# A conformer block on one core: another order of all steps, weight pieces that lie in one stretch, and 16 instead of 89 products of the unit matrix

## The chip, the core and the metric

The kernel runs on one core of one Trainium2 chip. The metric is device time in microseconds, as the median of several executions. The core has a matrix engine (TensorE, PE in the profile; its weight loads are PEld), a vector engine (VectorE, DVE), a scalar engine (ScalarE, ACT), GpSimd (POOL) and SyncE (SP), which issues all DMA transfers here. Each engine works through its own queue in order and waits for the others by semaphores.

## The reference

There are two parts. The first is attention in chunks of 32 positions, with 16 positions of left and 8 of right context and 8 memory keys for each head; the second is a gated feed-forward layer that mixes along the sequence.

```python
# attention: B, H, S, D = 4, 8, 768, 64
for c in range(24):                       # chunks of 32
    k_full = concat(mem_k, k[:, :, 32*c - 16 : 32*c + 40])    # cut at the ends
    v_full = concat(mem_v, v[:, :, 32*c - 16 : 32*c + 40])
    a = softmax(q_c @ k_full.T / 8)
    out[:, :, 32*c : 32*c + 32] = a @ v_full
x = out as (B, S, 512)
# feed-forward
h = gelu(x @ w_in)                        # 512 -> 1024, tanh form
u, v = h[..., :512], h[..., 512:]
v_n = (v - mean(v)) / sqrt(var(v) + 1e-6) * g_ln
v_s = einsum('ts,bsd->btd', w_sg, v_n) + b_sg      # along the sequence
return x + (u * v_s) @ w_out
```

The weights `w_in` and `w_out` reach the kernel as float64, w_sg as float32.

## The kernel before

**Tiles.** The 4 x 768 positions are cut into 24 tiles of 128 positions (four chunks), counted by `u` = 6 b + tt. One attention tile handles all eight heads. Three tiles make a half of a batch entry (384 positions). Products of the second part run in a split form: each operand is a pair of a rounded high part and the rest, and each product adds lo x hi, hi x lo and hi x hi (`product`), so three matmuls for each 128 x 128 block.

**Steps.** The code first defines all work as named steps in a table, each with its engine, or with two engines of which a star behind the name chooses the second. It then issues them in the order that the text `ORDER` gives. Each engine's queue, SP's included, holds its steps in just this order. A second text thus moves everything at once. The steps are:

- `q`, `k`, `v` + u: loads of a tile's queries, keys and values (SP). There are two buffers of q and of k, and three of v; a load waits until the last reader of its buffer is done.
- `S`: 64 matmul records that make the scores. `mx`, `sb`, `ex`, `sm`, `sa`, `sr`, `nm`: the softmax: maximum, subtraction (VectorE), exponential (ScalarE), sum, a small addition, reciprocal (VectorE), scaling (VectorE or GpSimd). `z` sets to zero the keys that lie outside (GpSimd).
- For the first ten tiles `T` (four transpositions on TensorE with the unit matrix) and `p` (the copy to `pt`) turn the weights around; for the others `yt` does so in blocks on VectorE, and the exchanges `Ea` to `Ed`, four transfers of 32 KB each within the chip's memory, move the blocks for two tiles at a time.
- `A`: 64 matmul records that weigh the values. `xc`, `xh`, `xl`: the copy to float32 (ScalarE), the high part (ScalarE), the rest (GpSimd or VectorE).
- `V`: the product with the second half of `w_in` for a tile (12 matmuls of 512 columns); `v1` to `v9` with `vx`, `vy`: gelu, statistics, normalisation (`v7`), the pair `vh` (`v8` on ScalarE, `v9` on GpSimd or VectorE).
- `U` + b, half, j: the product with a fourth of the first half of `w_in` (12 matmuls of 384 columns); `u1` to `u4`: its gelu.
- `W`: the product along the sequence (18 matmuls of 384 columns); it needs all six `vh` of the batch entry. `w1` to `w4`: shift, gate, the pair.
- `O`: the product with `w_out` (12 matmuls); `o1` adds x; `out` stores 192 KB.

**Weights.** A piece of `w_in` is 128 rows of 512 float64. `ri10` to `ri13` load those of the half that V needs, `ri00` to `ri03` those that U needs, `ro0` to `ro3` those of `w_out`. The steps `d1` to `d9` turn a piece into a pair of float32: `d1`, `d2` take the bits of the mantissa and the exponent apart (VectorE), `d3`, `d4` convert them (ScalarE), `d5`, `d6` add the low word and the sign (VectorE), `d7` multiplies (GpSimd or VectorE), `d8` rounds to the high part (ScalarE), `d9` subtracts it (GpSimd or VectorE). Six raw buffers serve the eight pieces of `w_in`. A V needs the pairs of all four `i1` pieces, a U those of all four `i0` pieces. `g` + st, half loads a piece of the transposed w_sg into one of seven buffers (`us`), which the U's use later; `ga` and `gb` make its pair. `cb` loads g_ln and b_sg, `cbh` halves them.

**Banks.** Four banks of PSUM (`mms`) serve T, V, U, W, O in turn; a step takes the one that has been free the longest. A V or a U holds its bank until its last gelu step. The scores and the weighted values have two banks each of their own.

**The unit matrix.** A step `zz7` issues `warm(7)`: seven products of the unit matrix with itself, into the bank that is next to be taken. Nothing reads what they write. A product of float32 is two matmul records in the profile.

**Line numbers.** All steps go through one helper, so nearly all instructions in the profile have the line L110. They are told apart by their tiles: `rawa` to `rawf`, `ma`.., `exa`.. belong to the pieces, `ea`, `eb`, `mx`, `rd` to the softmax, `paira`, `pairb` to x or to the gated product of the first and the second half, `ga`, `gb` to V, `ua` to `ug` to U and to pieces of w_sg, `vha` to `vhf` to the six vh.

Of the kernel before, what the change touches and what calls it, by code (L numbers as in the profile page):

```python
# [36 lines left out]
d2i10 g50 d5i01 d4i10 g40 sm0 S1 d6i10 g51 sa0 zz12 d7i01* g41 sr0 mx1 d8i01 d1i10 sb1 d3i10 k3 nm0 ex1
d5i10 T0 sm1 S2 p0 d9i01* A0 sa1 k4 mx2 q3 d2i12 ri11 sb2 zz12 d4i12 q4 d1i12 ex2 sr1 d6i12 d3i12 nm1* sm2
xh0 xc0 sa2 xl0 T1 d5i12 zz3 sr2 d7i10* p1 S3 nm2 d8i10 d7i12* A1 q5 d9i10* d8i12 ri13 T2 d1i11 xc1 k5 d2i11
zz9 d3i11 d9i12 mx3 xh1 p2* d4i11 sb3 xl1 S4 ex3 d5i11 zz22 d2i13 d1i13 d4i13 d6i11 d3i13 d6i13 ri03 ri00  # L40
d5i13 v2 d7i11* v4 d7i13 mx4 d8i11 sm3 sb4 d9i11 d8i13 sa3 S5 ex4 sr3 d9i13* zz2 k7 d1i03 V01 q7 mx5 nm3*
d3i03 k6 sm4 ri02 d2i00 v3 sa4 d2i03 d4i00 sr4 d5i03 d4i03 d6i00 T3 v101 A2 d6i03 p3 nm4* v201 V00 sb5 v5
xh2 q6 v301 xl2 d7i03 ex5 v401 xc2 d1i00 z5 d8i03 d1i02 d3i00 d2i02 T4 d9i03* v100 V02 sm5 d3i02 p4 v200
d4i02 d5i02 v300 sa5 d6i02 v400 A3 d7i02 sr5 v501 S6 v500 xc3 d8i02 nm5 A4 xh3 d9i02* T5 mx6 xl3 xc4 zz4 xh4
vx01 vx00 sb6 p5 V03 vy00 xl4 ex6 v600 vy01 d5i00 z6 v601 sm6 d7i00 sa6 sr6 A5 v701 d8i00 nm6 v801 V04 v700
xc5 v901* xh5 d9i00 v102 xl5 v800 v202 ga50 v900* v302 U001 gb50* v104 v402 g21 ga31 v204 ga40 gb31 ga41
v502 U003 v304 gb40* g01 ga51 gb41 v404 k8 u1001 v6 ga11 vx02 u2001 ga21 gb51 ro0 vy02 v504 T6 u3001 q8
u1003 S7 cb u4001 v602 ga20 vx04 gb21 u2003 p6 U000 vy04 mx7 ga01 v604 u3003 sb7 gb20 u4003 ex7 V05 v704
u1000 sm7 v804 gb11* v904* sa7 v702 v103 sr7 S8 u2000 v802 nm7* v203 u3000 U011 u4000 k10 v303 v902 mx8 k9
q9 v403 g00 cbh sb8 v105 g10 T7 u1011 v503 q10 U010 ex8 v205 p7 vx03 sm8 v305 vy03 u2011 U002 v405 u3011  # L50
v603 sa8 u4011 ga00 v505 ga10 gb00 sr8 vx05 S9 vy05 v605 v703 g30 A6 mx9 gb10 v7 v803 k11 U012 sb9 xc6 q11
nm8* u1010 ex9 u2010 v903* u3010 T8 ga30 v705 S10 d1o0 v805 gb30* d3o0 A7 u4010 v905 u1012 sm9 U013 u2012
xc7 sa9 p8* u3012 u4012 d2o0 d5o0 d4o0 W001 mx10 d6o0 sb10 d7o0 ro1 sr9 ex10 gb01* d8o0 W003 nm9* w1001
u1013 sm10 u2013 d9o0 w2001 u3013 sa10 w3001 u4013 sr10 w4001* W010 w1003 u1002 d1o1 u2002 d3o1 w2003 u3002
d5o1 w3003 d2o1 u4002 w4003 T9 d4o1 w1010 W002 d6o1 w2010 d7o1 ro2 p9* v8 w3010 nm10 d8o1 w4010 W012 w1002
w2002 d9o1 w3002 d2o2 d1o2 d4o2 w4002 W011 d3o2 w1012 d6o2 d5o2 w2012 ro3 d7o2* w3012 w4012 d8o2 A8 w1011
w2011 S11 xc8 d9o2* W000 w3011 mx11 q13 v9 w4011* d1o3 d2o3 d3o3 sb11 d4o3 d5o3 ex11 W013 d6o3 z11 w1000
d7o3* w2000 d8o3 yt10 w3000 d9o3* A9 w4000* w1013 O000 sm11 w2013 sa11 w3013 sr11 nm11* O002 o1000 w4013*
yt11 Eb5 O011 o1002 O012 o1011 Ec5 O001 o1012 v10 O010 o1001 out001 Ea5 O003 o1010 k13 O013 q12 o1003 xh7
xh6 out003 xl7* xh8 v11 xl6 out000 V11 v12 o1013 k12 xl8* out002 Ed5 V12 v111 v211 out011 v311 v411 U101  # L60
v511 v112 vx11 v212 xc9 vy11 v312 v611 V10 xh9 v412 u1101 v711 u2101 v811 v512 u3101 v911 u4101 vx12 S12
vy12 xl9* v612 v110 A10 v712 k14 v210 q14 v812 V13 mx12 xc10 v310 v912* xh10 v410 xl10* sb12 V14 v113 v510
ex12 v213 z12 vx10 v313 sm12 v413 A11 sa12 vy10 v513 v610 sr12 vx13 v710 S13 xc11 vy13 nm12 v613 U100 v810
mx13 xh11 v910* sb13 xl11 v114 yt12 U103 ex13 v214 u1100 v713 v314 sm13 v813 U113 v414 u1103 v913 sa13 u2100
sr13 u2103 u3100 nm13* v514 u3103 V15 u1113 u4100 u4103 u2113 yt13 u3113 vx14 u4113 Ed6 vy14 U111 v614 v115
v714 v215 v814 v315 v914 U110 u1111 v415 u2111 v515 u3111 U112 u4111 u1110 vx15 vy15 u2110 v615 u3110 v715
u4110 S14 v815 u1112 v915* U102 q16 mx14 q15 u2112 Ea6 sb14 u3112 u4112 W113 ex14 sm14 sa14 out012 sr14 nm14
Eb6 W103 w1113 w2113 out013 w3113 v13 w4113 out010 k15 u1102 W110 v14 w1103 Ec6 u2102 w2103 u3102 w3103
u4102 w4103 k16 W101 w1110 w2110 w3110 w4110 yt14 S15 w1101 A12 w2101 q17 mx15 w3101 k17 W112 w4101* xc12
sb15 ex15 sm15 sa15 sr15 W100 nm15* w1112 w2112 yt15 w3112 w4112* W111 w1100 w2100 w3100 w4100* S16 w1111  # L70
A13 w2111 mx16 w3111 W102 w4111 Ec7 xc13 sb16 ex16 sm16 sa16 sr16 k18 nm16* v16 S17 w1102 Eb7 O110 w2102
mx17 w3102 w4102* sb17 Ea7 O103 ex17 o1110 z17 sm17 sa17 sr17 O111 o1103 nm17* q19 k19 out103 v15 O113 q18
o1111 out111 Ed7 O101 o1113 O102 o1101 yt16 S18 o1102 A14 yt17 mx18 O100 xc14 sb18 ex18 z18 A15 sm18 xh12
o1100 xh14 S19 sa18 xl12* xh13 Ec8 sr18 xl14 O112 mx19 sb19 xl13 ex19 out110 V22 o1112 nm18* out102 sm19 v17
Ea8 sa19 sr19 nm19 U202 v122 v222 out101 Ed8 v322 U200 v422 u1202 u2202 v522 u3202 q20 u4202 V21 Eb8 u1200
vx22 vy22 v622 u2200 v722 u3200 u4200 v822 v922 v18 U201 v121 out100 q21 v221 v321 U203 v421 u1201 yt18 v521
u2201 V20 xc15 yt19 u1203 vx21 xh15 vy21 u2203 v621 u3201 xl15* u3203 u4201 A16 u4203 v120 v721 v220 v821
V23 v19 xc16 v921* k21 v320 k20 xh16 v420 out112 xl16 v520 A17 vx20 v123 vy20 v620 v223 V24 Ec9 xc17 v720
v323 xh17 v423 v820 xl17 v523 v20 vx23 S20 vy23 v920 Ed9 U210 mx20 v623 v124 sb20 v224 ex20 Ea9 S21 v723
v324 sm20 v823 V25 v424 u1210 v923 sa20 u2210 sr20 v524 u3210 out113 nm20* q22 u4210 k23 vx24 mx21 k22 U212  # L80
v125 vy24 sb21 Eb9 v624 v225 ex21 v724 v325 sm21 U213 v824 v425 u1212 v924 sa21 u2212 v525 u3212 U211 sr21
u1213 u4212 nm21* vx25 u2213 vy25 yt20 u3213 v625 u4213 A18 v725 yt21 v825 S22 v21 xc18 v925 A19 mx22 sb22
W211 Ec10 xc19 ex22 sm22 sa22 sr22 nm22 Ed10 W202 w1211 Ea10 W203 w1202 w2202 w3202 q23 Eb10 w4202* u1211
u2211 W210 w1203 u3211 w2203 v22 u4211 w3203 w2211 w4203 w3211 W213 w4211* w1210 yt22 w2210 w3210 w4210*
W201 w1213 w2213 w3213 w4213* W212 w1201 w2201 w3201 w4201* W200 w1212 w2212 w3212 w4212* O213 w1200 w2200
w3200 w4200 O212 o1213 O201 o1212 out212 O203 o1201 O211 o1203 S23 o1211 A20 mx23 O200 sb23 xc20 ex23 z23
sm23 O202 o1200 sa23 out200 sr23 nm23 out211 yt23 A21 xh20 o1202 xh18 xl20 out202 O210 xh19 xl19* xl18 V32
o1210 out210 out203 Ec11 U301 v132 v232 v23 v332 out201 V30 v432 u1301 Ed11 u2301 v532 u3301 u4301 vx32 vy32
v632 Ea11 U300 v130 v732 xc21 v230 v832 v330 v932 U303 u1300 v430 Eb11 xh21 u2300 xl21 v530 u3300 V31 u4300
u1303 vx30 vy30 u2303 v630 u3303 v730 u4303 v830 v930* V33 v131 v231 v331 v431 A22 v531 v133 vx31 v233 U302  # L90
xc22 vy31 v631 v333 xh22 v731 v433 v831 xl22 A23 u1302 v533 u2302 v931 V34 vx33 xc23 vy33 u3302 v633 xh23
u4302 v733 xl23* v833 v933 V35 v134 v234 v334 v434 U310 v534 v135 vx34 v235 vy34 v335 v634 U312 v435 u1310
v734 v535 v834 u2310 v934 U313 vx35 u1312 vy35 u3310 u2312 v635 u4310 u3312 v735 U311 u4312 u1313 v835 u2313
v935* u3313 u4313 W310 W312 w1310 w2310 w3310 w4310 u1311 W302 w1312 u2311 w2312 u3311 w3312 u4311 w4312*
W301 w1302 w2302 w3302 w4302 W311 w1301 w2301 w3301 w4301* W300 w1311 w2311 w3311 w4311 W303 w1300 w2300
# [536 lines left out]
```

## Time and profile before

| what | value |
|---|---|
| median of 3 runs | 406.43 us (404.9 to 407.65) |
| the profiled execution's own time | 406.15 us |
| its span, first to last instruction | 404.4 us |
| mean granted TensorE clock in it | 0.987 |
| busy: PE, DVE, ACT, POOL | 95%, 70%, 39%, 26% of the span |
| read and written | 36.96 MB, 6.29 MB |

The profile is of one execution. Busy time of PE is from modelled ends of pipelined matmuls, and the unit matrix counts in it. A row of the timeline gives start and duration in microseconds, engine, line, operation, tiles and shapes; a wait in square brackets is the idle time of that engine before the instruction and what ended it. A row of the chain of waits gives start, duration and what was on the chain. A row of the waits gives who waited for whom, the total, the number of times and the longest. A row of DMA issues gives the number of transfers, the size of one and the median time from issue to landing.

### The profile page before, as it was taken

Reading aid. Unit: us, or ns where it says so; the run is one execution under the profiler, and the core shown is the slowest. Engines: PE = TensorE matmul, PEld = TensorE weight load, DVE = VectorE, ACT = ScalarE, POOL = GpSimd, SP = SyncE. Lnnn points to the kernel's source line nnn. Section 1 sums busy time; section 2 is a strip of 40 time slices with the busy share of each in tenths; the row PEclk is TensorE's granted clock in tenths of the full one; section 3 lists DMA queues with packets and bytes.
Section 4 is the critical chain, followed back from the end, with each engine's and each line's share of the span. In section 5 each row is a group of like instructions: output and inputs, shape, how many; then the busy total and the mean of one; then the engine's idle time right before and its main releaser. Section 6 shows DMA issues by size and latency. Waiting matters only on the chain.

```text
span 404.4 us, 11378 instructions
## 1 busy us (share of the span) xinstructions
PE 384.9 (95%) x4922; PEld 358.3 (89%) x4922; DVE 283.5 (70%) x557; ACT 159.4 (39%) x296; POOL 106.0 (26%) x114
## 2 busy tenths in 40 slices
...
PEclk9699999999999999999999999998999999999999
...
GB/s 250 369 210 202 347 4 109 202 235 60 105 134 20 192 197 65 2 75 227 109 98 200 42 171 161 177 141 86 99 0 21 62 146 18 2 1 0 2 5 172
DMA packets 24530, 47.67 MB, mean 118 GB/s; under 512 B 4384, under 2 KB 13600, under 8 KB 24480
## 3 DMA queue, kind: packets, MB, share of 16 engines
...
q8 instruction: 39, 0.64, 0.6%
q14 instruction: 11, 0.09, 0.1%
HBM read 36.96 MB, written 6.29 MB: 107 GB/s over the span
## 4 chain that ended last, share of the span: by engine, by line
PE 64%; DVE 13%; DMA 10%; SPq 4%; ACT 3%; POOL 3%; issue 2%; DVEq 0%; ACTq 0%; POOLq 0%
PE mmb L110 16%; PE mmd L110 15%; PE mma L110 13%; PE mmc L110 13%; SPq L110 4%; PE av L110 4%; PE s L110 3%; DMA rawa<-in_w_in 2%; DMA pt<-y 2%; DVE ga L110 2%; DVE gb L110 2%; DMA rawf<-in_w_in 2%; DMA out<-xa 2%; DMA vb<-in_vs 1%; DVE rda L110 1%
## 5 line engine op out<-in xcount | busy, mean ns | idle before, releaser
L110 PEld LDWEIGHTS av<-pt,vb 64*64 64x64 f32 x512 | 8.7, 135 | 7.3 <-issue 3.4
L110 PE MATMUL av<-pt,vb 64*64 64x32 f32 x512 | 9.8, 221 | 5.6 <-issue 2.6
L110 PE MATMUL s<-kb,qb 64*32 64x64 f32 x768 | 10.6, 231 | 3.6 <-DVE rda L110 3.6
L110 PE MATMUL mma<-ident 128*128 128x128 f32 x74 | 12.7, 348 | 1.4 <-POOL mhalf L110 1.4
L110 DVE SCALAR_TENSOR_TENSOR gb<-gb,mmb 128x512 f32<-128x512 f32 x14 | 9.6, 683 | 6.1 <-ACT gb L110 6.1
L110 PEld LDWEIGHTS s<-kb,qb 64*32 64x32 f32 x768 | 8.6, 109 | 5.7 <-DVE rda L110 3.8
L110 PEld LDWEIGHTS mma<-ident 128*128 128x128 f32 x74 | 12.0, 257 | 1.6 <-POOL mhalf L110 1.4
L110 PEld LDWEIGHTS s<-ka,qa 64*32 64x32 f32 x768 | 8.7, 109 | 4.5 <-DVE gb L110 1.6
L110 PE MATMUL s<-ka,qa 64*32 64x64 f32 x768 | 10.5, 230 | 1.9 <-DVE gb L110 1.2
L110 ACT COPY xa<-av 128x512 f32<-128x512 f32 x9 | 5.3, 585 | 15.7 <-PE av L110 14.5
L110 ACT ACTIVATE ga<-ga 128x512 f32<-128x512 f32 (+1 forms) x14 | 8.9, 634 | 6.4 <-DVE ga L110 6.4
L110 ACT COPY xb<-av 128x512 f32<-128x512 f32 x9 | 5.3, 585 | 14.8 <-PE av L110 13.3
L110 DVE SCALAR_TENSOR_TENSOR mmd<-mmd,g_half,b_half 128x384 f32<-128x384 f32 x8 | 5.0, 624 | 8.4 <-PE mmd L110 8.4
L110 PE MATMUL mmb<-pairb,w_out_hi 128*128 128x384 f32 x56 | 10.9, 336 | 0.0
L110 ACT ACTIVATE gb<-gb 128x512 f32<-128x512 f32 (+1 forms) x14 | 8.8, 631 | 4.9 <-DVE gb L110 4.9
L110 POOL TENSOR_TENSOR rsb<-rsb,mhalf 128x1 f32<-128x1 f32 x8 | 4.6, 578 | 23.1 <-DVE rsb L110 23.1
L110 DVE SCALAR_TENSOR_TENSOR mmc<-mmc,g_half,b_half 128x384 f32<-128x384 f32 x9 | 5.6, 619 | 6.8 <-PE mmc L110 6.8
L110 PEld LDWEIGHTS av<-pt,vc 64*64 64x64 f32 x512 | 8.3, 134 | 2.3 <-issue 0.7
L110 PE MATMUL mmb<-w_in_hi,pairb 128*128 128x512 f32 x32 | 9.1, 404 | 1.4 <-POOL pairb L110 1.4
L110 ACT ACTIVATE eb<-eb 128x512 f32<-128x512 f32 x12 | 7.6, 630 | 6.3 <-DVE eb L110 6.3
L110 DVE TENSOR_REDUCE mxa<-s 128x8 f32<-128x512 f32 x8 | 5.4, 678 | 6.4 <-PE s L110 6.4
L110 PEld LDWEIGHTS av<-pt,va 64*64 64x64 f32 x512 | 8.4, 134 | 1.6 <-issue 1.0
(557 smaller groups left out, 1287.3 us busy)
## 6 DMA issues: line engine op xcount, KB each, us to landing
...
vb<-in_vs SPq DMA_DIRECT2D x8, 512.0 KB, 4.3
va<-in_vs SPq DMA_DIRECT2D x8, 512.0 KB, 5.5
vc<-in_vs SPq DMA_DIRECT2D x8, 512.0 KB, 4.7
pt<-y SPq DMA_DIRECT2D x112, 32.0 KB, 2.3
...
```

The costliest lines, as they stand in the source:

```text
L110: return self.tc.keep_in_program_order(getattr(self.engine, name)(*args, **kw))
```

## The change

There are four edits.

1. The host lays out `w_in` as (2, 4, 128, 512) words of 64 bits and w_sg transposed as (2, 6, 128, 384), so that each piece that one transfer loads lies in one stretch of memory. Before, a piece was a window of a wider matrix: rows of 4 KB at a distance of 8 KB for `w_in`, rows of 1.5 KB at a distance of 3 KB for w_sg. Sizes and the places in the core's memory stay the same. `w_out` stays as it was; its pieces already lay in one stretch.
2. `ORDER` holds the same 1292 steps in another order. The choice of engine changes for 38 steps that get a star and 26 that lose theirs; VectorE then has 569 in place of 557 instructions.
3. The steps `zz` are five with 16 products in all, in place of nine with 89.
4. `warm` issues nothing where no bank is free at that place of the order.

The start of the two orders, in the queues of the engines that the prediction speaks of:

```text
SP before:  k0 q0 g20 ri01 g11 ri10 q1 k1 k2 v1 v0 q2 g31 ri12 g50 g40 g51 g41 k3 k4 q3 ri11 q4 q5 ri13 k5 ri03 ri00
SP after:   ri11 ri01 q0 ri13 g50 q1 g11 ri12 k0 k1 v1 g20 k2 ri10 g31 g41 v2 q2 v0 ri00 q3 k3 k4 ri02 k5 q4 ri03 v4 cb
  later:    v3 q5 g30 k6 q6 v6 v7 k8 v5 q8 q7 g10 g51 k7 g01 q9 q10 k10 g40 g21 v8 k9 g00 ro0
DVE before: mx0 d2i01 sb0 d1i01 d6i01 d2i10 d5i01 sm0 d6i10 sa0 d7i01 sr0 mx1 d1i10 sb1 nm0 d5i10 sm1 d9i01 sa1 mx2
DVE after:  d1i11 d2i11 d5i11 d2i01 d6i11 d1i01 d7i11 d6i01 d5i01 d9i11 d1i13 d2i13 d1i12 d5i13 d2i12 d6i13 d5i12 d6i12
            mx0 sb0 d9i13 mx1 sm0 sb1 d2i10 sa0 sr0 sm1 sa1 sr1 d6i10 d1i10 mx2 sb2 d5i10 d1i00 sm2 sa2 sr2 d2i00 nm2
            xl0 mx3 p2 sb3 d2i02 d9i10
PE before:  zz7 S0 zz18 S1 zz12 T0 S2 A0 zz12 T1 zz3 S3 A1 T2 zz9 S4 zz22 S5 zz2 V01 T3 A2 V00 T4 V02 A3 S6 A4 T5 zz4
            V03 A5 V04 U001 U003 T6 S7 U000 V05 S8 U011 T7 U010 U002 S9 A6 U012 T8 S10 A7 U013 W001
PE after:   S0 S1 zz7 S2 T0 zz2 T1 A0 zz2 S3 T2 A1 zz2 A2 V00 S4 V02 V01 T3 S5 A3 S6 T4 zz3 A4 V03 V04 T5 T6 A5
            U001 U003 A6 S7 U012 V05 U000 S8 U011 U002 U010 T7 U013 A7 S9 T8 W011
later PE before: V20 A16 V23 A17 V24 ... U211 A18 S22 A19 W211
later PE after:  S19 A16 U200 A17 V24 V23 ... U201 W203 A18 W200 A19 S20 W213
```

The diff, with the two texts cut:

```diff
 ORDER = """
-k0 q0 g20 zz7 ri01 g11 ri10 q1 k1 S0 zz18 k2 mx0 v1 d2i01 v0 sb0 d4i01 q2 d1i01 ex0 g31 d6i01 ri12 d3i01 z0
...
+ri11 ri01 q0 ri13 g50 q1 g11 ri12 k0 d1i11 d2i11 k1 d3i11 d4i11 d5i11 d2i01 v1 d6i11 d4i01 g20 d1i01 d7i11*
...
-            f"i{half}{kt}", w_in[kt * P:(kt + 1) * P, 1024 * half:1024 * half + 1024],
+            f"i{half}{kt}", w_in[half, kt],
...
-            eng.dma_start(us.take(key), w_sgT[st * P:(st + 1) * P, ts_])
+            eng.dma_start(us.take(key), w_sgT[th, st])
...
     def warm(n):
-        for _ in range(n):
+        for _ in range(n if mms.free else 0):
             tensor.matmul(mms.free[0][:, 0:P], ident, ident, start=True, stop=True)
...
+    w_in = np.ascontiguousarray(moe_w_in).view(np.int64).reshape(4, P, 2, 512).transpose(2, 0, 1, 3)
+    w_sgT = np.asarray(moe_w_sg).T.reshape(6, P, 2, HALF).transpose(2, 0, 1, 3)
     arrays = {
-        "qs": qs, "ks": ks, "vs": vs, "w_in": np.ascontiguousarray(moe_w_in).view(np.int64), "g_ln": moe_g_ln,
-        "w_sgT": np.asarray(moe_w_sg).T, "b_sg": moe_b_sg, "w_out": np.ascontiguousarray(moe_w_out).view(np.int64),
+        "qs": qs, "ks": ks, "vs": vs, "w_in": w_in, "g_ln": moe_g_ln,
+        "w_sgT": w_sgT, "b_sg": moe_b_sg, "w_out": np.ascontiguousarray(moe_w_out).view(np.int64),
     }
```

More of the change, by code (lines that the diff above doesn't have):

```diff
@@ L35 @@
 ORDER = """
-k0 q0 g20 zz7 ri01 g11 ri10 q1 k1 S0 zz18 k2 mx0 v1 d2i01 v0 sb0 d4i01 q2 d1i01 ex0 g31 d6i01 ri12 d3i01 z0
[L37 to L95, printed above, removed]
@@ L96 @@
-w3300 w4300* W313 w1303 w2303 w3303 w4303* O300 w1313 w2313 w3313 w4313 O303 o1300 O313 o1303 O312 o1313
-O310 o1312 out312 out213 O302 o1310 O311 o1302 out302 out303 out313 O301 o1311 out311 out310 out300 o1301
-out301
+ri11 ri01 q0 ri13 g50 q1 g11 ri12 k0 d1i11 d2i11 k1 d3i11 d4i11 d5i11 d2i01 v1 d6i11 d4i01 g20 d1i01 d7i11*
+d3i01 d6i01 d8i11 d5i01 d9i11* d1i13 d2i13 d3i13 d7i01 d4i13 d1i12 d8i01 d5i13 d3i12 d2i12 S0 d6i13 d4i12
+d5i12 k2 d6i12 ri10 g31 d7i13 mx0 g41 sb0 v2 d9i01 q2 d8i13 S1 v0 ex0 ri00 d9i13* z0 q3 zz7 k3 d7i12 mx1 sm0
@@ new lines @@
+sb1 d8i12 d2i10 ex1 d9i12 sa0 sr0 d4i10 sm1 sa1 nm0* sr1 S2 d6i10 d1i10 T0 nm1* k4 mx2 d3i10 zz2 p0 sb2
+d5i10 T1 ex2 A0 d1i00 ri02 d7i10 sm2 p1 d3i00 zz2 sa2 sr2 xh0 d2i00 S3 xc0 nm2 d8i10 xl0 T2 d4i00 k5 mx3 A1
+q4 p2* ri03 zz2 sb3 v4 xc1 d2i02 cb ex3 A2 d9i10* v3 d4i02 sm3 q5 V00 xh1 g30 d1i02 xc2 d6i00 d3i02 d6i02
+xh2 d5i02 xl1 xl2 S4 sa3 v100 sr3 d1i03 V02 d7i02 v200 k6 d3i03 q6 mx4 v300 d5i03 d8i02 nm3* sb4 v400 ex4
+V01 d9i02* v102 cbh v500 v202 vx00 sm4 v302 T3 vy00 v402 S5 sa4 v502 p3 sr4 A3 vx02 v600 mx5 nm4* vy02 sb5
@@ new lines @@
+v6 xc3 S6 ex5 d5i00 v602 xh3 T4 d2i03 z5 d7i00* zz3 d4i03 sm5 xl3 p4 mx6 d8i00 A4 sa5 v702 d9i00 sb6 V03
+v802 v7 sr5 xh4 k8 ex6 v902* v5 xc4 q8 z6 xl4 nm5* v101 q7 sm6 g10 v201 V04 sa6 d6i03 v301 sr6 v401 d7i03*
+nm6 d8i03 T5 v501 T6 d9i03* p5 p6* A5 ga50 ga30 vx01 gb50* ga20 U001 gb30* g51 ga31 gb20 vy01 k7 ga10 ga41
+g01 xc5 gb31* v601 ga11 v700 U003 xh5 v701 u1001 gb41 xl5 v801 u2001 ga51 gb11 v800 A6 u3001 v900* ga01
+u4001 v901 S7 u1003 v104 u2003 U012 xc6 mx7 q9 gb51 u3003 v204 v103 gb10 u4003 v304 v203 V05 u1012 gb01*
@@ new lines @@
+v303 v404 sb7 v504 ex7 v403 U000 vx04 u2012 v503 u3012 vy04 sm7 v604 u4012 S8 u1000 vx03 v704 U011 vy03
+u2000 v804 q10 v603 mx8 k10 u3000 v904 g40 sa7 u4000 g21 sb8 v8 U002 v105 v703 k9 u1011 sr7 v205 v803 nm7*
+u2011 v305 u3011 U010 v405 v903 ex8 u4011 v505 ga40 gb40 sm8 ga21 T7 vx05 sa8 vy05 U013 gb21* g00 v605 p7*
+ro0 u1002 sr8 u2002 v705 u3002 A7 nm8 v805 u4002 v905 S9 ga00 xc7 T8 gb00 mx9 W011 p8 sb9 u1010 d2o0 ex9
+d1o0 u2010 d4o0 sm9 d3o0 d6o0 u3010 W013 w1011 u4010 d5o0 w2011 ro1 d7o0* q11 w3011 v9 sa9 w4011 d8o0 sr9
@@ new lines @@
+W010 w1013 nm9 u1013 u2013 d9o0* u3013 u4013 d2o1 T9 w2013 d4o1 A8 d1o1 w3013 p9* d3o1 W003 d6o1 xc8 d5o1
+w1010 d7o1 ro2 w2010 w3010 w4013* d8o1 w4010 W002 w1003 d9o1* w2003 w3003 d2o2 d1o2 d4o2 w4003* W012 d3o2
+w1002 d6o2 d5o2 w2002 ro3 d7o2* k11 w3002 w4002 d8o2 S10 w1012 A9 w2012 k12 d9o2* w3012 q12 W000 mx10 w4012
+sb10 d2o3 ex10 d1o3 d4o3 sm10 d3o3 d6o3 S11 w1000 d5o3 W001 k13 w2000 mx11 w3000 d7o3* sb11 d8o3 w4000* ex11
+S12 d9o3* z11 w1001 O013 sm11 mx12 sa11 w2001 sr11 sa10 w3001 O011 nm11* sr10 o1013 nm10 w4001* O012 o1011
@@ new lines @@
+yt10 sb12 yt11 O001 ex12 o1012 Ec5 z12 sm12 sa12 sr12 O003 o1001 nm12* out013 q13 v11 O002 o1003 out003 k14
+q14 O000 o1002 S13 o1000 xh7 xh6 O010 xl7 mx13 xh8 sb13 xl8 ex13 S14 o1010 xl6* V12 out010 Ea5 sm13 mx14
+sa13 sr13 nm13 V10 Eb5 v112 v212 v312 v412 out002 U103 v512 v110 k15 q16 vx12 v210 Ed5 vy12 v310 v612 U102
+v410 u1103 u2103 v712 u3103 v10 v510 v812 q15 V11 u4103 u1102 out001 v912* out000 u2102 vx10 u3102 vy10 yt12
+v610 u4102 U101 v111 v710 sb14 v810 v211 ex14 v910* v311 U100 sm14 u1101 xc9 u2101 sa14 xh9 v411 u3101 sr14
@@ new lines @@
+A10 xl9* u1100 nm14* v511 V13 u4101 xc10 vx11 yt13 xh10 vy11 u2100 v611 u3100 xl10* u4100 A11 v711 v113 v811
+v213 V14 Ed6 xc11 v911* v313 xh11 v413 xl11* v513 Ec6 U110 v114 vx13 vy13 v613 v214 v713 v314 v813 V15 v414
+v12 u1110 v913 Ea6 v514 u2110 vx14 u3110 vy14 v614 u4110 U111 v714 v115 out012 v814 v215 out011 k16 v914
+v315 Eb6 U113 v415 u1111 u2111 v515 u3111 u4111 U112 u1113 vx15 vy15 v615 u2113 v715 u3113 u4113 v815 S15
+v915 yt14 A12 k17 mx15 W110 sb15 xc12 ex15 sm15 sa15 sr15 nm15 S16 w1110 yt15 W113 k18 mx16 v14 w2110 v13
@@ new lines @@
+sb16 w3110 w4110* ex16 u1112 sm16 W102 w1113 sa16 u2112 sr16 w2113 u3112 nm16* u4112 w3113 w4113* W112 w1102
+w2102 w3102 w4102* A13 w1112 w2112 W100 Ec7 xc13 w3112 w4112* q18 Ed7 W111 w1100 w2100 w3100 w4100* q17 v15
+W103 w1111 Eb7 w2111 w3111 w4111 Ea7 O111 w1103 w2103 w3103 w4103 O112 o1111 S17 o1112 yt16 A14 mx17 W101
+sb17 xc14 ex17 z17 sm17 sa17 sr17 nm17* S18 w1101 A15 w2101 yt17 w3101 O113 mx18 Ea8 w4101* sb18 ex18 O103
+o1113 z18 Ed8 sm18 sa18 sr18 nm18* O100 o1103 out103 O101 o1100 O102 o1101 out101 Ec8 O110 o1102 xh14 xh12
@@ new lines @@
+xl14* xh13 xl12* v17 xl13 V22 v18 o1110 v16 Eb8 U203 v122 out102 v222 k19 q19 v322 out100 V20 v422 u1203
+out110 u2203 v522 u3203 u4203 yt18 V21 vx22 v120 vy22 v622 v220 v722 v320 v822 v420 xc15 v922* S19 xh15 v520
+A16 v121 k21 xl15* vx20 U200 mx19 xc16 vy20 v221 xh16 v620 sb19 v321 xl16 ex19 v421 A17 u1200 sm19 V24 v720
+v20 xc17 v521 q20 v820 u2200 xh17 v920 vx21 sa19 u3200 vy21 sr19 u4200 nm19* V23 v124 v224 v621 xl17 yt19
+v324 Ed9 v424 v721 U210 v524 v821 vx24 v921 vy24 out111 V25 u1210 Eb9 v624 v123 u2210 v724 u3210 v223 v824
@@ new lines @@
+u4210 v323 v924* q21 U211 out112 v423 v125 Ea9 v523 v225 U212 u1211 vx23 vy23 v325 v623 u2211 v425 u3211 v19
+Ec9 v723 U202 v525 u1212 v823 u2212 vx25 v923* u3212 vy25 u4212 U213 v625 k20 u1202 u4211 out113 u2202 v725
+u3202 v825 u4202 U201 u1213 v925* u2213 u3213 W203 u4213 A18 w1203 w2203 W200 xc18 w3203 w4203* u1201 u2201
+u3201 A19 u4201 w1200 S20 w2200 xc19 W213 w3200 k22 mx20 w4200* sb20 ex20 sm20 S21 w1213 sa20 W212 w2213
+mx21 w3213 sr20 w4213* nm20 sb21 yt20 ex21 W210 w1212 sm21 w2212 sa21 w3212 sr21 nm21 w4212* W211 w1210 yt21
@@ new lines @@
+w2210 Ec10 w3210 w4210 W202 w1211 w2211 v21 Eb10 w3211 w4211 O211 w1202 Ed10 w2202 w3202 w4202* O213 o1211
+k23 Ea10 W201 o1213 q23 q22 O210 w1201 w2201 w3201 w4201 A20 o1210 S22 xc20 O200 mx22 sb22 ex22 O201 o1200
+sm22 sa22 sr22 nm22* S23 o1201 A21 out201 mx23 v22 yt22 O203 sb23 ex23 z23 O202 sm23 o1203 sa23 sr23 nm23
+O212 o1202 xh20 yt23 xh19 out202 xh18 out203 xl20* Eb11 xl19* V32 o1212 xl18 v23 out212 U302 v132 Ec11 v232
+v332 V31 v432 u1302 out213 u2302 out210 v532 u3302 out200 u4302 Ea11 vx32 vy32 v632 V30 v131 v732 v231 v832
```

9 lines of the change are left out of this document (added).

## The prediction, made before the result was known

> **What bounds the kernel now.** I read the page first, then the stretches, the chain of waits, VectorE's waits, single rows of the timeline.
>
> ```profile
> span 404.4 us, 11378 instructions
> ...
> PE 384.9 (95%) x4922; PEld 358.3 (89%) x4922; DVE 283.5 (70%) x557; ACT 159.4 (39%) x296; POOL 106.0 (26%) x114
> ...
> PEclk9699999999999999999999999998999999999999
> ```
>
> TensorE looks full, but that row counts the unit matrix and the waits inside a pipelined group. What the products need comes from pieces of the chain: in their order below a unit group, the scores S, the values A, a unit group, a transposition T, then V, U or O (12 matmuls of 384), W.
>
> ```profile
> 2.11 6.58 DMA rawf<-in_w_in
> 14.79 5.43 PE mma L110 x28
> 20.22 0.79 PE s L110 x53
> 21.01 1.06 PE av L110 x64
> 29.44 0.59 PE mmc L110 x4
> 32.83 5.11 PE mmd L110 x44
> 231.66 2.78 PE mmb L110 x12
> 359.34 3.12 PE mmd L110 x18
> 384.29 2.09 PE mmc L110 x12
> ```
>
> 24 S at 0.79, 24 A at 1.06, 10 T at 0.59, 24 V at 2.78, 64 U and O at 2.08 and 32 W at 3.12 are 350 us. The other 54 are the subject. The first V starts at 39.20 (row below), with 6 S, 2 A and 3 T done, 8.6 us: 30.6 lost. The first W starts at 93.86; the work between is 47.2 of 54.7 us: 7.5 lost. The remaining 310.5 hold 294.4 of work: 16.1 lost, 3.5 of it the last addition and store.
>
> ```profile
> 39.20 1.18 PE L110 MATMUL mmd<-w_in_hi,paira 128*128 128x512 f32 x4
> 93.86 0.33 PE L110 MATMUL mma<-w_sg_hi,vha 128*128 128x384 f32 x1
> ```
>
> So the start is what counts, and there VectorE sets the pace: it turns each float64 weight piece into two floats, beside softmax. The stretches (columns: PE, PEld, DVE, ACT, POOL busy, granted clock, DMA share, GB/s):
>
> ```profile
> 0.00:10.00 10.00, 8.60 (x114) 8.09 (x114) 1.98 (x4) 0.78 (x1) 0.77 (x8) 1.00 0.81 249
> 10.00:20.00 10.00, 6.38 (x92) 6.22 (x92) 7.74 (x17) 4.83 (x8) 0.19 (x1) 0.66 0.99 375
> 30.00:39.20 9.20, 9.19 (x196) 8.70 (x194) 9.10 (x15) 5.36 (x10) 4.98 (x5) 1.00 0.54 176
> ```
>
> VectorE is idle for 8 of the first 10 us and full from 30 on. Its waits in the first 95 us:
>
> ```profile
> DVE mxa L110 <- PE s L110: 6.4, 2, 5.9
> DVE mxc L110 <- PE s L110: 2.7, 2, 2.1
> DVE exf L110 <- DMA rawf<-in_w_in: 2.2, 1, 2.2
> DVE exf L110 <- ACT exf L110: 1.2, 1, 1.2
> DVE ua L110 <- ACT ua L110: 1.0, 1, 1.0
> ```
>
> **VectorE's queue, counted.** Starts of neighbours give the price of one when the queue is full: 0.60 for 512 columns of floats (27.99 to 28.59), 0.34 for an integer step (28.59 to 28.93), 0.11 for a small one (26.12 to 26.23), 0.47 for 384 columns (64.47 to 64.94).
>
> ```profile
> 26.12 0.20 DVE L110 RECIPROCAL rdc<-rdc 128x8 f32<-128x8 f32 x1
> 26.23 0.64 DVE L110 TENSOR_TENSOR ma<-ma,exa 128x512 f32<-128x512 f32 x1
> 27.99 0.68 DVE L110 TENSOR_TENSOR w_in_lo<-ma,w_in_hi 128x512 fp32r<-128x512 f32 x1
> 28.59 0.42 DVE L110 TENSOR_SCALAR mb<-rawb 128x512 int32<-128x512 int32 x1
> 28.93 0.42 DVE L110 TENSOR_SCALAR exb<-rawb 128x512 int32<-128x512 int32 x1
> 64.47 0.55 DVE L110 TENSOR_TENSOR w_sg_lo<-ud,w_sg_hi 128x384 fp32r<-128x384 f32 x1
> 64.94 0.68 DVE L110 SCALAR_TENSOR_TENSOR ga<-ga,mma 128x512 f32<-128x512 f32 x1
> ```
>
> Before the first V, the old order has 53 instructions on VectorE (to d9i13: 35 wide, 10 integer, 8 small), 25 us; the new one 47 (to d9i10: 28, 13, 6), 22 us. Up to v705, the last normalisation before W, the old order has 149 (85 wide, 18 of 384, 16 integer, 30 small), 68 us; the new one 148 (80, 22, 16, 30), 67 us. So the amount hardly moves; what moves is when it starts and how often it stops.
>
> ```profile
> 88.09 0.54 DVE L110 TENSOR_SCALAR ga<-ga,mvc,rsc 128x512 f32<-128x512 f32 x1
> 89.36 1.26 POOL L110 TENSOR_TENSOR vhf<-ga,vhf 128x512 fp32r<-128x512 f32 x1 [1.90 <-ACT vhf L110]
> 31.19 1.28 POOL L110 TENSOR_TENSOR paira<-xa,paira 128x512 fp32r<-128x512 f32 x1 [0.70 <-ACT paira L110]
> 31.27 1.74 DVE L110 SCALAR_TENSOR_TENSOR mb<-rawb,mb 128x512 f32<-128x512 uint32 x1
> ```
>
> The old v705 ends at 88.6, 20.7 after the bare sum. The waits above are 13.5; the other 7 are small waits and stretching beside GpSimd, as at 31.27, where a step of 0.68 took 1.74.
>
> **Part by part.** *Loads.* The first piece waited behind k0, q0 and g20, and took 6.58 us. Alone in the queue, a strided piece (rawd) and one that lies in one stretch (w_out) take:
>
> ```profile
> rawd<-in_w_in SPq DMA_DIRECT2D x1, 512.0 KB, 4.6
> y<-in_w_out SPq DMA_DIRECT2D x4, 512.0 KB, 3.3
> ```
>
> The new order issues ri11 first; at w_out's price from the first issue, about 0.7, it is there at 4.0, at rawd's at 5.3. I take 4.0, since w_out has the same rows of 4 KB and the new layout. [...] The later pieces arrive ahead of VectorE. k0 moves behind four pieces, so S0 starts near 12 instead of 4.7; its maximum has 18 instructions, 8.7 us, ahead of it on VectorE, so that is covered, though only just. w_sgT's pieces have hundreds of instructions of cover and I cost them at nothing. On SP's queue, ri10 stands behind k2, which waits for S0, and k7 behind g51, which waits for gb50. Who needs ri10 has 24 instructions ahead on VectorE (12.3 us), who needs k7 has 10 between gb50 and its own step (4.5 us): I cost both at nothing, and 2 us each if the cover is gone.
>
> *Unit matrix.* 89 products become 16. At 0.23 each (44 records in 5.11, two records a product) 73 are 17 us of TensorE, nearly all while it waited anyhow. One group was in the way: the 28 records from 14.79, at a half clock, held S2 and so the 2.1 us wait of mxc. The bounds of the removal are that gain of 2, and a loss from a colder clock (below); I take 1 us lost for the latter.
>
> *Order.* VectorE now starts at 4.0. Its waits, estimated: 1.6 for ScalarE's first answer (the table load, then d3), 2 for S1 and S2, 1.5 for the U's, as ua's row. With 7 for the rest, as GpSimd has 25 large operations there after 23, that is 16 in place of 20.7, from 11 to 21. v705 then ends at 67 + 16 = 83, and W follows when vhf is done, 2.0 later by the two rows at 88 and 89: 84.5. TensorE itself allows it: V00 at 22 + 9 = 31; of the 55 us of work that the new order has ahead of W (10 S, 8 A, 6 V, 8 U, 9 T) 4 S, 3 A and 3 T are done by then, 47 are left: 78. I take 84. Against 93.86 that is 9.9, less one S (0.79) that the new order has not done by then: **9 us**.
>
> *The later batches.* TensorE's waits after 95 us, and the W that ran cold after the idle time before it:
>
> ```profile
> PE av L110 <- ACT xa L110: 1.5, 1, 1.5
> PE mmb L110 <- POOL pairb L110: 1.4, 2, 0.8
> 275.52 4.78 PE mmd L110 x18
> ```
>
> A19 follows A18 with one S between, and waits for ScalarE to empty the bank; in the new order W200 stands between. The W behind it took 4.78 for 3.12. A V that follows its values at once waits for GpSimd; now a U or another V stands between, or VectorE does that step. Those are 4.5 us, less what new waits take: the exchanges stand between loads and stores on SP, with some 1 us of cover each at A12 and A14. I take **3 us**, from 4.5 gained to 5 lost.
>
> **Sum.** 404.4 - 9 - 3 = 392.4. The profiled execution was 406.15 for that span, 1.75 more: 394. Its 406.15 lies 0.3 under the median of 406.43, which I leave.
>
> **Rivals.** *The front gives back its gain.* The first piece comes early but VectorE loses the time again by waits for S0, k2 or GpSimd: W at 90, 3 us gained, nothing later: 403 at the most, 399 with the 3 later. For it: six edges above have under 1 us of cover. Against: a queue that starts 4.7 us earlier with the same work must lose them anew.
> *No change.* The front gains 9 and the exchanges lose it: A10, A12, A14, A16 each late by 2 us or so: 402 to 408. Against: the old order keeps S, A and E as near to each other.
> *The clock.* The row of 10 to 20 us shows it: TensorE waited 3.6 us, and the clock granted was 0.66; the 28 records cost 0.19 each there, 0.12 later. With 16 unit products left TensorE is idle up to S0. If the clock then stays at one half up to the first U, the work from V00 to there (5 V, 3 S, 4 T, 3 A, 22 us) takes 22 more, 3 of it hidden by VectorE: 413. It decides from about 16 us of work at one half. [...]
> *The change isn't what it says.* The loop makes no unit product where no bank is free, so even fewer than 16: nothing in time.
>
> **Numbers.** Forecast, 386 to 399: 0.66. Gain given back: 0.16, mostly faster still. No change: 0.10. Clock, or another loss: 0.08. The range of 386 to 403 takes in the bounds of the front (11 to 21 of lag) and the first rival. One per cent, 4 us, is about what a measurement can tell from no change: faster 0.79, same 0.12, slower 0.09.
>
> **What would show it.** VectorE's first weight step at 4 to 5 us; the first V at 29 to 33; the first W at 82 to 86; no PE wait for a value bank near the third batch's W; its clock low in one or two slices of the front and full later. I am wrong if VectorE's waits in the front add up to more than 10 us, if the first W comes after 90, or if TensorE waits for pt after 150 us.

## The result and the profile after

The changed kernel takes 394.66 us (median of 4, 393.48 to 394.84) beside 405.66 for the kernel before in the same comparison (4 runs, 404.07 to 407.65). The ratio is 0.9713, 95% interval 0.9673 to 0.9753. (A ratio, here and below, leaves out executions in a slower state, so it need not be the quotient of the medians.) The profiled execution took 393.48 us with a span of 391.7, against 406.15 and 404.4: 12.7 us less.

The page of the changed kernel, three lines:

```profile
span 391.7 us, 11059 instructions
...
PE 365.5 (93%) x4776; PEld 338.5 (86%) x4776; DVE 289.3 (74%) x569; ACT 160.5 (41%) x295; POOL 93.9 (24%) x103
...
PEclk9999999999999999999999999999999999999999
```

PE's busy time fell by 19.4 us (some 17 of them are the 73 unit products, by the prediction's price) and the span by 12.7: a busy share is no measure of what TensorE needs. The row of the clock looks perfect and isn't, as a later section shows.

The same landmarks in the timeline of the changed kernel (start, duration, instruction): VectorE's first weight step, the first V, the first W.

```profile
4.36 0.43 DVE L109 TENSOR_SCALAR mb<-rawb 128x512 int32<-128x512 int32 x1 [4.36 <-DMA rawb<-in_w_in]
```

```profile
33.49 1.19 PE L109 MATMUL mmd<-w_in_hi,paira 128*128 128x512 f32 x4
34.52 1.09 PE L109 MATMUL mmd<-w_in_lo,paira 128*128 128x512 f32 x4
```

```profile
85.40 0.42 PE L109 MATMUL mmd<-w_sg_hi,vha 128*128 128x384 f32 x1
```

The stretches of the changed kernel (PE, PEld, DVE, ACT, POOL busy, clock, DMA share, GB/s), and VectorE's longest waits in the first 95 us:

```profile
0.00:10.00 10.00, 0.00 (x0) 0.00 (x0) 5.28 (x11) 4.47 (x6) 1.44 (x9) 1.00 0.81 304
10.00:20.00 10.00, 4.05 (x136) 3.64 (x137) 8.98 (x14) 4.99 (x8) 6.44 (x6) 1.00 0.96 343
```

```profile
DVE mb L109 <- DMA rawb<-in_w_in: 4.4, 1, 4.4
DVE mxb L109 <- PE s L109: 0.7, 1, 0.7
DVE vha L109 <- ACT vha L109: 0.6, 1, 0.6
```

VectorE is busy for 5.3 of the first 10 us instead of 2.0, and TensorE does nothing at all in them. The old waits of 6.4, 2.7 and 2.2 us are gone; what is left behind the first piece is one of 0.7 and smaller ones.

TensorE's waits after 95 us were 4.8 us in five rows (1.5, 1.4, 0.9, 0.7, 0.3; the first two stand in the prediction). In the changed kernel they are 1.1 us in two:

```profile
PE av L109 <- ACT xc L109: 0.9, 1, 0.9
PE s L109 <- DMA qa<-in_qs: 0.2, 1, 0.2
```

To see where the gain arises, I take at each landmark the time less the work of the products issued by then, by the prices of the prediction (T at 0.50; good to 0.3 us). The e8 column starts with the same front as the one before, so their difference of about 1 us there shows how far two executions differ. "Batch 2" is the third of the four; e8 is an experiment below.

| lost up to | before | after | e8 |
|---|---|---|---|
| first V | 30.8 | 25.7 | 29.6 |
| first W | 38.8 | 31.1 | 37.7 |
| first V of batch 2 | 43.8 | 35.2 | 44.3 |
| first O of batch 2 | 49.7 | 37.4 | 46.5 |
| first O of batch 3 | 51.5 | 38.7 | 48.2 |

So 7.7 us of the gain are there at the first W, 8.6 at the first V of batch 2, 12.3 at its first O, and hardly more comes after it.

### The profile page after: what moved, and what is told of

Same layout as the page of the kernel before. It is cut to its first block, busy times and chain, and to the rows that moved or that the text cites. A ratio compares the mean times of both kernels' runs of the same rounds, so it can differ in the third digit from the quotient of the medians.

```text
span 391.7 us, 11059 instructions
## 1 busy us (share of the span) xinstructions
PE 365.5 (93%) x4776; PEld 338.5 (86%) x4776; DVE 289.3 (74%) x569; ACT 160.5 (41%) x295; POOL 93.9 (24%) x103
## 4 chain that ended last, share of the span: by engine, by line
PE 73%; DVE 13%; DMA 6%; SPq 3%; ACT 2%; issue 1%; POOL 0%; DVEq 0%; POOLq 0%
PE mma L109 17%; PE mmd L109 16%; PE mmb L109 16%; PE mmc L109 16%; PE av L109 5%; PE s L109 3%; SPq L109 3%; DMA rawc<-in_w_in 2%; DMA va<-in_vs 1%; DVE gb L109 1%; DMA ug<-in_w_sgT 1%; DVE ga L109 1%; DVE ea L109 1%; DMA qa<-in_qs 1%; DMA qb<-in_qs 1%
## 5 line engine op out<-in xcount | busy, mean ns | idle before, releaser
L109 POOL TENSOR_TENSOR pairb<-ue,pairb 128x384 fp32r<-128x384 f32 x3 | 3.1, 1024 | 41.4 <-ACT pairb L109 27.1
L109 ACT ACTIVATE ea<-ea 128x512 f32<-128x512 f32 x12 | 7.6, 632 | 12.8 <-DVE ea L109 12.7
L109 POOL TENSOR_TENSOR rsc<-rsc,mhalf 128x1 f32<-128x1 f32 x8 | 5.0, 631 | 31.2 <-DVE rsc L109 31.2
L109 DVE SCALAR_TENSOR_TENSOR mmb<-mmb,g_half,b_half 128x384 f32<-128x384 f32 x9 | 5.6, 618 | 9.3 <-PE mmb L109 9.3
L109 DVE SCALAR_TENSOR_TENSOR mma<-mma,g_half,b_half 128x384 f32<-128x384 f32 x8 | 5.0, 623 | 7.6 <-PE mma L109 7.6
L109 PE MATMUL av<-pt,va 64*64 64x32 f32 x512 | 9.5, 220 | 0.9 <-ACT pt L109 0.8
L109 POOL TENSOR_TENSOR rsa<-rsa,mhalf 128x1 f32<-128x1 f32 x8 | 4.4, 552 | 24.0 <-DVE rsa L109 24.0
L109 PE MATMUL av<-pt,vc 64*64 64x32 f32 x512 | 9.4, 220 | 0.7 <-DMA vc<-in_vs 0.6
L109 PE MATMUL mmc<-paira,w_in_hi 128*128 128x384 f32 x48 | 9.3, 336 | 0.0
```

The lines of the kernel that those rows point to most:

```text
L109: return self.tc.keep_in_program_order(getattr(self.engine, name)(*args, **kw))
```

## The experiments

**The layout alone** (e1 in the new order, e6 in the old). The edit of e1 (the host's two arrays change to match); e6 is the reverse in the kernel before:

```diff
-            f"i{half}{kt}", w_in[half, kt],
+            f"i{half}{kt}", w_in[kt * P:(kt + 1) * P, 1024 * half:1024 * half + 1024],
-            eng.dma_start(us.take(key), w_sgT[th, st])
+            eng.dma_start(us.take(key), w_sgT[st * P:(st + 1) * P, ts_])
```

> The changed kernel, with the weight pieces as windows of the wider matrices again. If the layout makes a piece land sooner, as the prediction took it (1.3 us for the piece that VectorE waits for first), the first piece lands at 5.5 to 7 us instead of 4.3, VectorE's first step moves with it, all of the front follows, and the time is 396 to 397.5 against 394.7. If a distance of 8 KB between rows costs nothing, the first piece lands at 4.4 and the time stays within 0.7 of 394.7.

> The old order with its 89 products and the new layout, nothing else. The run of the two orders spliced had this front, and there the first piece landed at 6.6 us instead of 8.7, the first V started at 35.7 instead of 39.2 and the first W at 88.9 instead of 93.9. If the layout did that, the first piece lands at 6.6 again and the time is 400 to 402. If the late landing of 8.7 belonged to the one profiled execution of the kernel before, the time stays within 1 us of it, 404.5 to 406.

e1 took 395.24 us (ratio to before 0.9734, 0.9692 to 0.9776), 0.6 more than the changed kernel, inside the interval. VectorE's wait for the first piece in e1:

```profile
DVE mb L109 <- DMA rawb<-in_w_in: 4.8, 1, 4.8
```

So 4.8 against 4.4 us, and the first W comes at 86.2 against 85.4. In the old order the first piece, which stands behind other loads there, lands at 7.8 us with the new layout (e6; 6.6 in e4 below, which has the same front) and at 8.3 to 8.8 us without it (before, e5, e7, e8). e6 took 404.35 (0.9967, 0.9925 to 1.0009): not told apart from no change; neither case of its expectation came. In the new order the layout is worth 0.4 us at the first piece, not the 1.3 that I had charged, and the times don't show it.

**The unit products alone** (e2: the new order with no `zz` step; e5: the old order with none).

```diff
-... z0 q3 zz7 k3 ... d3i10 zz2 p0 ... p1 d3i00 zz2 sa2 ... ri03 zz2 sb3 ... d7i00* zz3 d4i03 ...
+... z0 q3 k3 ... d3i10 p0 ... p1 d3i00 sa2 ... ri03 sb3 ... d7i00* d4i03 ...
```

> The changed kernel without its 16 remaining products of the unit matrix. If VectorE sets the pace of the front and TensorE's clock matters little there, the time stays within 1 us of 394.7 and the first V starts within 1 us of 33.5. If the products are what opens the clock, the S, T, A and the first V run at half speed for another 3 to 7 us, the first V starts after 35 and the time is 396.5 to 398. If they stand in the way, as a group did before the change, the first V starts before 33 and the time is up to 1 us less.

> The kernel before without its 89 products of the unit matrix. By the prediction's step the group ahead of S2 cost VectorE 2.1 us, so without it the first part gets shorter; the run without the 16 products showed the other side: the clock opened at 40 us instead of 22 and the first W came 3.3 us later. If both hold here they about cancel: within 2 us of the kernel before. If the products only hinder, it is 2 to 4 us faster; if they only keep the clock open, 2 to 5 us slower, with the first V at half clock.

e2 took 395.93 us (0.9749, 0.9704 to 0.9793), 1.3 over the changed kernel; in the profiled execution (span 394.5) the clock opened only at 40.2 us, and A2 and the first V ran cold. A2 in the changed kernel, then A2 and the first rows of V in e2:

```profile
32.12 1.45 PE L109 MATMUL av<-pt,vc 64*64 64x32 f32 x64
```

```profile
33.29 1.94 PE L108 MATMUL av<-pt,vc 64*64 64x32 f32 x64 [0.70 <-ACT xa L108]
35.15 2.07 PE L108 MATMUL mmd<-w_in_hi,paira 128*128 128x512 f32 x4
37.02 1.91 PE L108 MATMUL mmd<-w_in_lo,paira 128*128 128x512 f32 x4
```

Four matmuls take 2.07 and 1.91 where the changed kernel's took 1.19 and 1.09. The first V came 1.7 us late already, and the first W 3.3. Up to T2 (29.60 against 29.68) e2 isn't late at all: where the seven unit products stood, TensorE waits 3.0 us ahead of S2, but S2 starts at 21.28, before the changed kernel's 21.53, right behind the landing of its queries at 21.19. What follows at half the clock (A1, A2, the first V) makes the delay. So in this trace the 16 products are worth about 3 us at the first W; the 1.3 us between the medians lie within the intervals. e5 took 404.94 (0.9971, 0.9932 to 1.0011). There the 89 products are both help and hindrance: without them the first W comes at 90.9 instead of the 92.8 to 93.9 of the three traces that have them and the old layout (before, e7, e8), though the clock is low (stretches as above, e5):

```profile
20.00:30.00 10.00, 5.96 (x189) 5.00 (x184) 9.25 (x20) 6.73 (x12) 3.41 (x3) 0.72 0.73 243
30.00:40.00 10.00, 4.86 (x134) 3.97 (x135) 9.97 (x18) 4.48 (x8) 5.04 (x4) 0.50 0.63 220
```

The two to three microseconds don't show in the time, which differs from the kernel before's by less than its interval.

**The kernel before once more** (e7, no edit), for a second trace of it.

> The kernel before, profiled once more. If the slow first piece comes from rows at a distance of 8 KB, it lands at 8 to 9 us again, the first V starts at 39 and the first W at 94. If it was that execution's own, it lands at 6.5 to 7, the first V starts at 36 to 37 and the first W at 89 to 91, and the span differs from 404.4 by less than that.

One execution, 409.02 us, span 407.2. Its waits of TensorE from 195 to 300 us begin with two:

```profile
PE s L110 <- DMA qa<-in_qs: 1.7, 1, 1.7
PE av L110 <- ACT xa L110: 1.5, 1, 1.5
```

The second is A19's, as in the prediction. The first is S18's: the load of q18 stands behind seven steps on SP's queue, from v16 to v15, two exchanges and a store among them, that wait for work of their own. The trace quoted in the prediction has 0.7 us there under another name, though q18 landed at 223.13 and S18 began at 223.27:

```profile
PE s L110 <- DMA pt<-y: 0.7, 1, 0.7
```

Behind it e7's clock falls to one half from 226.7 to 230.1 us. The executions of the old order up to here (before, e5, e6, e7) all lose in these two places.

**The two halves of the order spliced** (e3: new order up to the first V of batch 2, then the old one; e4: the reverse; both with the new layout). The edit is the text `ORDER`, cut ahead of V22, with the steps already issued left out of the rest.

> The new order up to the first V of the third batch, then the old order for what is left (S19 with its softmax a little later than there); the new layout. In the two profiles the new order gains 8.6 us up to that place and 4.1 behind it. If the two gains are independent, the time is about 394.7 + 4 = 399 and the waits of the third batch come back: the first W of that batch cold or late, by 3 us. If the later gain only follows from arriving there with a lead on VectorE, the old rest keeps most of it and the time is 395 to 396.5.

> The old order with its 89 products of the unit matrix up to the first V of the third batch, then the new order for what is left; the new layout. If the gains are independent, the old front costs 8.6 us: about 403 less what the layout gives the old front (0 to 3), so 400 to 403, and from the third batch on no wait over 1 us of TensorE. If the later gain hangs on the lead, the time is 404 to 406.

e3 took 402.16 (0.9884, 0.982 to 0.9948), e4 406.19 (1.0005, 0.9977 to 1.0033). If the two parts simply added up, they would come to about 398 and 402; e3 is above both cases of its expectation. But both traces lose at the seam. e4 has the first of these rows (A16, which waits 0.9 in the changed kernel), e3 the second (V23, which waits 0.3 in the kernel before).

```profile
PE av L108 <- ACT xc L108: 5.1, 1, 5.1
```

```profile
PE mmc L108 <- DVE pairb L108: 2.0, 1, 2.0
```

(e3's trace is of its longest execution, 405.0 us; whether the other three wait there is not shown.) The splices tell nothing of what each part is worth; an order cut in two is a third order.

**Two places of the old order** (e8). The old order, old layout, 89 products, and only this: xc18 and q18 move forward, and v925 goes to VectorE.

```diff
-... A18 v725 yt21 v825 S22 v21 xc18 v925 A19 ...
+... A18 xc18 v725 yt21 v825 S22 v21 v925* A19 ...
-... k18 nm16* v16 S17 ... O113 q18 o1111 ...
+... k18 q18 nm16* v16 S17 ... O113 o1111 ...
```

> The order, layout and unit matrix of before, with two places altered behind the second batch: ScalarE empties A18's bank (xc18) right behind A18 instead of behind v825 (VectorE takes v925 in its place), and the load of q18 stands right behind that of k18 on SP's queue. Theory that these two waits are the later gain of the new order: A19 no longer waits 1.5 us for ScalarE, S18 no longer 0.7 to 2.0 us for q18, the W or O behind them does not run at half clock (1.7 us each); 401 to 404 us, 3 to 5 under the kernel before, first V of batch 2 to first W of batch 2 within 1 us of the new order's loss. Rival, that any gap closed there opens elsewhere: the two waits go, and the time is that of before within 1 us.

402.79 us (0.9936, 0.9899 to 0.9974): 2.5 less than the 405.33 of the kernel before there, by the interval 1.1 to 4.1. TensorE's waits from 195 to 300 us in e8:

```profile
PE mmb L108 <- POOL pairb L108: 0.8, 1, 0.8
PE av L108 <- DMA pt<-y: 0.7, 1, 0.7
PE mmc L108 <- DVE pairb L108: 0.2, 1, 0.2
```

Both waits are gone, and nothing has taken their place. In the table above, e8 loses 2.2 us from the first V of batch 2 to its first O, just as the changed kernel does (37.4 less 35.2), where the kernel before loses 5.9 and e7 5.1. So by the traces these two places are the whole of what the new order gains there. The gain shows in the time: 402.79 lies within the 401 to 404 expected, but 2.5 us is less than the 3 to 5 expected. What each of the two is worth alone was not run.

**GpSimd's work in the front on VectorE** (e9). Eleven wide steps get the other engine:

```diff
-d7i01 d7i13 d9i01 d7i12 d9i12 d7i10 d7i02 xl1 nm0* nm1* nm3*
+d7i01* d7i13* d9i01* d7i12* d9i12* d7i10* d7i02* xl1* nm0 nm1 nm3
```

> The changed kernel with eleven wide steps of the front (d7, d9 of three pieces, d7 of two, the rest of tile 1, three softmax scalings) on VectorE instead of GpSimd. VectorE gets 6.6 us more work there. If GpSimd's wide steps stretch VectorE's beside them, by 5.8 us up to 40 us in the profile of the changed kernel, nearly all of it is given back: the first V within 1.5 us of 33.5 and the time 393.5 to 396. If GpSimd's work is free for VectorE, the first V starts 5 us later or more and the time is 398 to 401.

395.31 us (0.9723, 0.9657 to 0.9789), the same as the changed kernel; first W 85.3. In the changed kernel's timeline one step of VectorE beside two of GpSimd:

```profile
14.01 1.75 DVE L109 SCALAR_TENSOR_TENSOR exc<-rawc,exc 128x512 int32<-128x512 int32 x1
```

```profile
13.56 1.65 POOL L109 TENSOR_TENSOR md<-md,exd 128x512 f32<-128x512 f32 x1 [1.90 <-DVE exd L109]
15.17 1.71 POOL L109 TENSOR_TENSOR w_in_lo<-mf,w_in_hi 128x512 fp32r<-128x512 f32 x1
```

and the same step in e9, where VectorE has taken those over:

```profile
13.59 0.69 DVE L108 SCALAR_TENSOR_TENSOR exc<-rawc,exc 128x512 int32<-128x512 int32 x1
```

1.75 us became 0.69. Summed over the front (each step's time less the usual one of its kind), stretching fell from 9.0 to 3.4 us while VectorE took on 6.6 us of work: 5.6 gained for 6.6 paid. In this front 6.6 us of wide steps given to GpSimd save VectorE only 1.0.

**The first piece later** (e11). The new order with three loads moved ahead, as the old order has them:

```diff
-ri11 ri01 q0 ri13 g50 q1 g11 ri12 k0 d1i11 ... d4i01 g20 d1i01 ...
+k0 q0 g20 ri11 ri01 ri13 g50 q1 g11 ri12 d1i11 ... d4i01 d1i01 ...
```

> The new order, but with the loads of k0, q0 and the table's scales (g20) issued ahead of the first weight piece, as before. Theory that the front gain hangs on when VectorE's first weight step starts: it starts at 6.3 to 7.0 instead of 4.4, and first V, first W and the time come 2 to 2.5 us later, 396.7 to 397.5 us. Rival, that the earlier k0 makes up for it, since TensorE's clock opens earlier and S0 comes at 5: 394 to 395.5 us.

400.62 us (0.988, 0.9817 to 0.9943), all four between 399.7 and 402.7: 6.0 more than the changed kernel for a start of VectorE at 6.81 instead of 4.36. The direction was right and the size was not. The rows of TensorE, then of VectorE, show what the theory on record missed:

```profile
34.56 1.01 PE L108 MATMUL av<-pt,vc 64*64 64x32 f32 x54
38.35 0.63 PE L108 MATMUL av<-pt,vc 64*64 64x32 f32 x10 [2.78 <-issue]
38.91 2.07 PE L108 MATMUL mmd<-w_in_hi,paira 128*128 128x512 f32 x4
```

```profile
40.17 0.69 DVE L108 SCALAR_TENSOR_TENSOR ma<-rawa,ma 128x512 f32<-128x512 uint32 x1 [2.64 <-ACT ma L108]
...
44.83 0.69 DVE L108 SCALAR_TENSOR_TENSOR ga<-ga,mmd 128x512 f32<-128x512 f32 x1 [2.05 <-ACT ga L108]
```

In the middle of A2, 54 of its 64 records done, TensorE stops for 2.78 us with nothing to wait for that the profile shows. ScalarE's queue has A2's copy ahead of the conversion `ma`, so VectorE waits 2.64. The clock falls to one half from 36.9 to 43.7 us, V00 runs at 2.07 for four matmuls, and VectorE waits another 2.05 for its gelu. 2.45 of later start, 2.64 and 2.05 are 7.1; the first W came 7.0 later (92.4). So in this trace only 2.45 of the 7.0 come from the start itself; the rest hangs on where that pause fell.

**A warm TensorE from the start** (e10), and that with the eleven steps of e9 (e12):

```diff
-... d3i12 d2i12 S0 d6i13 ...
+... d3i12 d2i12 zz36 S0 zz16 d6i13 ...
```

> The new order with 36 unit products ahead of S0 and 16 behind it, so that TensorE is busy from its start. Theory that the cold clock in the first 22 us costs nothing but the 0.7 us wait of mxb: the clock opens before 12 us, 394 to 395 us. Rival, that the clock before the first V is worth the 1 us that the prediction charged, or more: 392.5 to 393.5 us. If the unit products stand in the way of S0 or S1: 396 us.

> The 52 unit products of the run before and the 11 wide GpSimd steps of the front on VectorE, together. If either removes what keeps the other from paying (VectorE waits for nothing in the front, and no step of it is stretched): first W at 84 or earlier and 392 to 393.5 us. If VectorE's amount of work alone sets the front: 394.5 to 395.5 us, as the eleven steps alone.

394.83 us (0.9734, 0.9677 to 0.9791) and 394.42 (0.9715, 0.9666 to 0.9764): neither can be told from the changed kernel. The unit products of TensorE, in the changed kernel, then in e10:

```profile
18.25 3.35 PE L109 MATMUL mma<-ident 128*128 128x128 f32 x14
```

```profile
13.14 3.84 PE L108 MATMUL mma<-ident 128*128 128x128 f32 x32
```

0.24 us a record against 0.12: in the changed kernel TensorE is cold until 22 us, in e10 it isn't, and the first W comes at 85.4 and 85.3. A cold clock in the first 22 us costs nothing here, since VectorE sets the pace. Then e10 loses 1.8 us where the changed kernel loses nothing, within its first W, which lasts 5.1 us in place of 3.4:

```profile
87.45 0.34 PE L108 MATMUL mmd<-w_sg_hi,vhc 128*128 128x384 f32 x1 [1.56 <-ACT ua L108]
```

This is the third of six matmuls of one kind, and the operand it shares with the others has long been there; the row puts the idle time down to ScalarE's `ua`, which no matmul of W reads. The section on the hardware says what it is. So I know of no version better than the changed kernel.

## Why the prediction was right, and where its sum was not

The forecast of 394 us was 0.7 off, and its mechanism held: VectorE paced the start, began 4.35 us earlier and did not lose that again. But that the sum came so near is luck: two errors cancelled in it. The front gave 7.7 us for the 9 forecast, the later batches 5.0 for 3.

- *First piece.* Forecast 4.0 us, landed at 4.33; VectorE began at 4.36. Right; the layout's share in it was 0.4 us, not 1.3 (e1).
- *The lag of 16 us behind the bare sum of 67.* The last normalisation before W ended at 84.06, so the lag was 17.1. Its parts were other than assumed: 4.4 for the first piece, 3.6 of waits (5.1 had been set for three of them alone), and 9.0 of stretching (5.6 of it went in e9, with GpSimd's steps). Stretching had been put into "7 for the rest" on the strength of one row; it grew from 5.4 to 9.0, as I read it because GpSimd's wide steps now lie beside a VectorE that hardly rests. e9 shows that moving these eleven steps doesn't buy it back. (The prediction's list of VectorE's waits also passes over a row of 1.2 us, for `ud`, which so lies in its "other 7"; and the work behind the first W adds up to 294.2, not 294.4, which enters nothing.)
- *The first W.* 83 and 2.0 make 85, but the text went on with 84.5 and then 84. Measured: 85.40. That slip in the adding, not the mechanism, is most of the 1.3 us between 9 and 7.7. (The longer lag was made up here: W began 1.3 behind the normalisation in place of 2.0, since only its sixth matmul reads the last `vh`.)
- *First V at 29 to 33:* it came at 33.49, just outside, with 4.4 us of the stretching ahead of it.
- *Later batches.* Of the 4.5 us named there (A19, its cold W, the waits for `pairb`) all went. New waits took 1.1 in place of the 1.5 allowed, and by ScalarE's copy rather than by the exchanges. What was not priced were three shorter rows of the same list, 0.7, 0.9 and 0.3: the first is S18's wait, which in e7 is 1.7. With them the sum is 4.5 + 1.9 - 1.1 = 5.3, against 5.0 measured. e8 confirms the places of A19 and S18.
- *Unit matrix and clock.* The charge of 1 us for the colder clock was wrong: e10 is warm and its first W comes only 0.1 us earlier. Without the products that remain the clock is still low when the first V comes, and that trace's first W comes 3.3 us later (e2); the times don't tell it from nothing. The sign "its clock low in one or two slices of the front" isn't on the page, whose record starts late; by the unit products' duration it was low there up to about 22 us. The rival of a clock low up to the first U did not happen; e2 shows how near it was, with an opening at 40.2 us. In the changed kernel's trace the clock opened at 22.0 us, 3.7 after the seven unit products began at 18.25 and 4.9 after S1 did. In the kernel before's it closed at 12.4 us, 2.4 into a wait that began at 9.98, until 19.2, and at 275.2, 0.9 after the end of a wait of 1.53 us, until 278.6.
- *S0, ri10, k7 at nothing.* Right: the scores' first maximum began at 15.7 with VectorE's queue full ahead of it, and no wait of VectorE's or TensorE's for ri10 or k7 is above 0.2 us.
- *The rivals.* "The front gives back its gain" is what e11 did, by a path that I had not named: 2.45 us of later start became 7.0 at the first W. The changed kernel doesn't show it.
